# Folding the width once more ahead of a Fourier kernel's first product, in a new order of steps

## The chip, the cores and the metric

One core of one Trainium2 chip. The metric is the device time of one execution in microseconds (us); smaller is better. The engines are named as the profile names them: PE (TensorE, matrix products), DVE (VectorE), ACT (ScalarE), POOL (GpSimd) and SP (SyncE, which here only issues loads).

## The reference

Two heads stand side by side in the output. Head A filters an image of 2048 x 512 in the frequency domain; head B is an FNet layer, the real part of a two-dimensional Fourier transform by given matrices.

```python
# A: x (1, 2048, 512), w_r and w_i (2048, 257)
X = jnp.fft.rfft2(x, axes=(-2, -1))
a = jnp.fft.irfft2(X * (w_r + 1j * w_i), s=(2048, 512), axes=(-2, -1))
# B: x (1, 2048, 512), four DFT matrices given as inputs
p = jnp.einsum("bsd,ed->bse", x, dft_hid_re)
q = jnp.einsum("bsd,ed->bse", x, dft_hid_im)
b = jnp.einsum("ts,bse->bte", dft_seq_re, p) - jnp.einsum("ts,bse->bte", dft_seq_im, q)
return jnp.concatenate([a, b], axis=-1)
```

All values are fp32.

## The kernel before

Both transforms are done by products with tables of cosines and sines, and symmetries halve them. For B the kernel uses its own tables, and it reads the given matrices (34 blocks of 1 MB) only to compare them with what they should be; if one differed, a slow path after the main part (`tc.If`) would compute B from the given matrices.

Each piece of work is a named step. A string, `PLAN`, lists all steps in one order, written out by hand; the instructions of PE, DVE, ACT and SP are issued in exactly that order, each engine taking its own steps from it and waiting by semaphores for the others. POOL's stores are not in the manual order: they are issued as soon as what they store is ready, in their own order. The steps:

- A's input: `xa` loads a block of x (SP), transposed so that the width (512) lies on the partitions, as two halves of two parts k of 128. There are eight blocks i of 256 rows, two to a buffer (b = i // 2, c = i % 2). `fold{i}` (DVE, lines 333 to 339) adds and subtracts the two halves (d and d + 256) into `us`; fold0 and fold1 do one block each, fold3, fold5 and fold7 two. `hid{i}` (PE, L347) is the first product, over the width: h = 0 for even and h = 1 for odd frequencies, the two parts k added up in PSUM, for two groups r of 128 rows. Each `mm` of fp32 is run as two passes (a weight load and a matmul each). `zs{i}` (ACT) copies its result out of PSUM, `f16_{i}` (PE, L359) is a transform of length 16 along the sequence, `ys{i}` (ACT) copies that to `fz`.
- A's spectrum, eight slots n, for each: `w` (SP, weights and table), `tr` (PE transposes, L405), `ez` (ACT), `sf` (DVE, L415 to L417), `fwd` (PE, L424 or L428), `prod` (DVE, the product with the weights, L455 to L459), `comb` (DVE, L463 to L467), `inv` (PE, L485 or L488), `ev` (ACT). Slot 2 is a special one (g2, sx2, spec2, spy).
- A's output, eight steps j: `hi` (PE, L520), `eu` (ACT), `g16_` (PE, L532), `sc` (ACT), `eo` (DVE, two instructions, L541), and one store `st` (POOL, L547, 1 MB) for two j.
- B: `xb` loads, `xr` (ACT), `al` (PE, L606 and L607), `av` (ACT), `bh` (PE, L628 to L632), `hv` (ACT), `ro` (PE, L644), `y1` and `y3` (ACT), `y2` (DVE, L659), `pt` (POOL stores); `rx` and `ry` for one row.
- The comparison: `tt` loads a table (1 MB, two buffers), `cl{i}` loads a block of the given matrix (1 MB), `cc{i}` compares (DVE, one instruction of 128 x 2048, L701; cc16 and cc17, for the hidden matrices, four of about 512 each), `sg` (ACT) flips signs in a table between its uses. Each compare leaves a sum in `stat`; after the last step these are added up (`rs`, `pf`, `flag`), and all engines read `flag`.

The blocks that xa, xb and cl load into share one ring of six buffers (`blk`, NB = 6) of 1 MB: a load waits on SP until the block six before it in the order is no longer needed. PSUM holds three tiles of the kind `pa` for A and two of the kind `pb` for B, in the same way.

Of the kernel before, what the change touches and what calls it, by code (L numbers as in the profile page):

```python
# [16 lines left out]
P = 128  # L17
# [125 lines left out]
def _tables():  # L143
# [63 lines left out]
    first = np.concatenate([hf.reshape(2, 128, 512).transpose(1, 0, 2).reshape(128, 1024),  # L207
                            f16.reshape(128, 128), np.eye(128)], 1)
# [15 lines left out]
def kernel(  # L224
# [52 lines left out]
    dve.memset(ones, 1.0)  # L277
    zero = sp.tile([P, 512], mybir.dt.bfloat16, name="zero")
# [31 lines left out]
    def us(b):  # L310
        return part(2048 * (b % 2), 2, 2, 2, 256)

    def forward(i):
# [6 lines left out]
        if i < 4 or c:  # L320
            @step(f"xa{i}")
            def _():
                if c == 0 or i > 3:
                    block(("xs", b))
                if i < 4:
                    load(xs(b)[:, c], xa[0, :, i].rearrange("p r k f -> p r (k f)"))
                else:
                    load(at["xs", b], xa[0, :, i - 1 : i + 1].rearrange("p c r k f -> p (c r k f)"))

        if i < 2 or c:  # L330
            @step(f"fold{i}")
            def _():
                for h, op in enumerate((ADD, SUB)):
                    if i < 2:
                        TT(out=us(b)[:, h, c].rearrange("p k f -> p (k f)"), in0=xs(b)[:, c, 0], in1=xs(b)[:, c, 1],  # L335
                           op=op)
                    else:
                        TT(out=us(b)[:, h].rearrange("p c k f -> p c (k f)"), in0=xs(b)[:, :, 0],  # L338
                           in1=xs(b)[:, :, 1], op=op)

        @step(f"hid{i}")
        def _():
            pd = bank_a(("pd", i))
            for r in range(2):
                for h in range(2):
                    for k in range(2):
                        mm(pd[:, r, h], us(b)[:, h, c, k, 128 * r : 128 * r + 128], hf[:, k, h],  # L347
                           start=k == 0, stop=k == 1)
# [159 lines left out]
    def inverse(j):  # L508
# [35 lines left out]
        if half:  # L544
            @step(f"st{quad}")
            def _():
                pool.dma_start(out_a.rearrange("(r p) s -> p r s", p=P)[:, :, 512 * quad : 512 * quad + 512],  # L547
                               ob.rearrange("p r k g s -> p (r k) (g s)"))
# [227 lines left out]
    dve.tensor_reduce(out=rs, in_=stat, axis=mybir.AxisListType.X, op=ADD)
    pf = bank_b("pf")[:, :1]
    mm(pf, ones, rs, start=True, stop=True)
# [122 lines left out]
```

## Time and profile before

| what | value |
|---|---|
| time, median of 3 runs | 205.94 us (204.54 to 206.11) |
| the profiled execution | 205.54 us |
| its span in the profile | 203.4 us |
| PE busy | 182.2 us (90%) |
| DVE busy | 155.6 us (76%) |
| ACT busy | 83.6 us (41%) |
| POOL busy | 23.0 us (11%) |
| moved by DMA | 66.24 MB, mean 326 GB/s |
| granted clock of PE, mean | 0.961 |

How to read it: an instruction's row names its line in the kernel, its engine, and output <- input. PE's own time is not the sum of its instructions' durations, since they overlap; the distance between two starts is what one costs. The chain of waits goes back from the end of the execution to whatever released each instruction, and so names what set the time. A granted clock of 1.00 is PE's full clock; 0.50 is half of it.

### The profile page before, as it was taken

The numbers are of one execution on the slowest core, as the hardware profiler recorded it, in microseconds if no ns is written. First come the engines' busy times: TensorE is split into PE (matmuls) and PEld (weight loads), VectorE is DVE, ScalarE is ACT, GpSimd is POOL, SyncE is SP. The second block draws the span as 40 slices with busy tenths as digits, with TensorE's granted clock in tenths as the row PEclk, the third lists the DMA queues.
The fourth block names the chain that finished last, engine by engine and source line by source line (L and its number), as shares of the span: only waits on it lengthen the run. The fifth ranks groups of instructions, "written<-read, shape, count | busy, mean of one in ns | idle before, by whom it ended". The sixth has DMA issues, their size and how long they took to land.

```text
span 203.4 us, 2751 instructions
## 1 busy us (share of the span) xinstructions
PE 182.2 (90%) x1017; PEld 156.5 (77%) x1017; DVE 155.6 (76%) x217; ACT 83.6 (41%) x114; POOL 23.0 (11%) x32
## 2 busy tenths in 40 slices
PE   7299999999999999898999995799999999999810
PEld 2189999999996998788956853777787999999700
DVE  0454049915997899999999999946499997999770
ACT  2003555677864356425332352154344436141400
POOL 5000000000100000000000022303352423101010
PEclk9999999999999999999999999599999999999965
DMA  6999999999999996779599029398999999999241
GB/s 197 396 417 412 427 376 421 401 413 406 398 413 405 407 388 233 255 270 358 148 337 338 29 58 356 153 338 310 428 352 395 367 416 421 421 419 414 114 174 47
DMA packets 19603, 66.24 MB, mean 326 GB/s; under 512 B 1760, under 2 KB 2656, under 8 KB 18688
## 3 DMA queue, kind: packets, MB, share of 16 engines
q1 hardware_dynamic: 16784, 56.33, 72.4%
q0 software_dynamic: 2656, 9.08, 11.4%
q10 hardware_dynamic: 144, 0.59, 0.9%
q8 instruction: 10, 0.16, 0.3%
q14 instruction: 9, 0.07, 0.1%
HBM read 57.61 MB, written 8.39 MB: 325 GB/s over the span
## 4 chain that ended last, share of the span: by engine, by line
PE 58%; DVE 34%; DMA 3%; issue 2%; POOL 0%; ACT 0%; DVEq 0%; ACTq 0%; POOLq 0%
PE pa L347 15%; PE pa L520 14%; DVE work L459 9%; DVE blk L701 8%; PE pa L532 7%; PE pa L359 7%; DMA wsp_sb<-in_wsp 3%; PE pb L644 3%; DVE work L463 3%; DVE work L465 3%; PE pb L632 3%; DVE work L466 2%; DVE work L464 2%; PE pa L485 2%; DVE work L415 2%
## 5 line engine op out<-in xcount | busy, mean ns | idle before, releaser
L701 DVE SCALAR_TENSOR_TENSOR blk<-blk,tt 128x2048 f32<-128x2048 f32 (+2 forms) x24 | 41.4, 1754 | 2.8 <-ACT tt L741 2.3
L701 DVE SCALAR_TENSOR_TENSOR blk<-blk,odd,tt 128x2048 f32<-128x2048 f32 x16 | 37.1, 2346 | 6.6 <-DMA blk<-in_cm 6.6
L347 PE MATMUL pa<-ta,work 128*128 128x256 f32 x128 | 31.1, 401 | 3.7 <-DVE work L335 3.7
L347 PEld LDWEIGHTS pa<-ta,work 128*128 128x128 f32 x128 | 25.4, 203 | 8.1 <-DVE work L335 4.6
L520 PE MATMUL pa<-ta,fz 128*128 128x256 f32 x128 | 29.5, 386 | 0.0
L520 PEld LDWEIGHTS pa<-ta,fz 128*128 128x128 f32 x128 | 28.9, 305 | 0.4 <-issue 0.2
L485 PE MATMUL pa<-fi,work 128*128 128x128 f32 x112 | 15.8, 300 | 4.8 <-DVE work L467 3.8
L485 PEld LDWEIGHTS pa<-fi,work 128*128 128x128 f32 x112 | 14.8, 211 | 6.0 <-DVE work L467 4.2
L459 DVE TENSOR_TENSOR work<-pa,w 128x1024 f32<-128x1024 f32 x14 | 16.5, 1219 | 2.3 <-PE pa L424 1.6
L352 ACT COPY work<-pa 128x1024 f32<-128x1024 f32 x8 | 8.1, 1012 | 24.1 <-PE pa L347 24.1
L363 ACT COPY fz<-pa 128x1024 f32<-128x1024 f32 x8 | 15.3, 1942 | 3.6 <-PE pa L359 3.6
L338 DVE TENSOR_TENSOR work<-blk 128x1024 f32<-128x1024 f32 x6 | 7.1, 1221 | 12.7 <-PE pa L347 12.7
L525 ACT COPY work<-pa 128x1024 f32<-128x1024 f32 x8 | 8.1, 1013 | 20.8 <-PE pa L520 20.8
L359 PEld LDWEIGHTS pa<-ta,work 128*128 128x128 f32 x128 | 15.4, 192 | 0.4
L359 PE MATMUL pa<-ta,work 128*128 128x128 f32 x128 | 15.4, 275 | 0.0
L532 PEld LDWEIGHTS pa<-ta,work 128*128 128x128 f32 x128 | 15.1, 192 | 0.2
L532 PE MATMUL pa<-ta,work 128*128 128x128 f32 x128 | 15.1, 275 | 0.0
L541 DVE TENSOR_TENSOR work<-pa,work 128x512 f32<-128x512 f32 x16 | 10.3, 684 | 6.2 <-ACT work L536 6.2
L606 PE MATMUL pb<-fb,blk 128*128 128x200 f32 (+1 forms) x64 | 14.6, 309 | 0.0
L607 PE MATMUL pb<-fb,xr 128*128 128x200 f32 (+1 forms) x64 | 14.6, 309 | 0.0
L492 ACT COPY fz<-pa 128x1024 f32<-128x1024 f32 x8 | 8.1, 1011 | 12.6 <-PE pa L485 9.5
L424 PE MATMUL pa<-work,fi 128*128 128x512 f32 x28 | 12.8, 592 | 0.0
(94 smaller groups left out, 240.7 us busy)
## 6 DMA issues: line engine op xcount, KB each, us to landing
blk<-in_cm SPq DMA_DIRECT2D x32, 1024.0 KB, 11.1
tt<-tab_tt SPq DMA_DIRECT2D x4, 1026.0 KB, 15.4
w<-in_wa SPq DMA_DIRECT2D x8, 512.0 KB, 9.2
out_a<-work POOLq DMA_DIRECT2D x4, 1024.0 KB, 8.6
blk<-in_xb SPq DMA_DIRECT2D x15, 256.0 KB, 7.9
blk<-in_xa SPq DMA_DIRECT2D x4, 512.0 KB, 7.2
blk<-in_xa SPq DMA_DIRECT2D x2, 1024.0 KB, 11.1
blk<-in_wd SPq DMA_DIRECT2D x2, 1024.0 KB, 6.8
```

Source lines behind the costliest of these rows:

```text
L347: mm(pd[:, r, h], us(b)[:, h, c, k, 128 * r : 128 * r + 128], hf[:, k, h], start=k == 0, stop=k == 1)
L359: mm(y[:, r, c], zs[:, r, 128 * c : 128 * c + 128], f16, start=True, stop=True)
L363: act.copy(fz.rearrange("p c k (n g) -> p g (c k n)", g=16)[:, i::8], flat(at["py", i]))
L424: mm(flat(px[:, h]), ft[:, 0], flat(t[:, h]), start=True, stop=True)
L459: TT(out=m[:, h].rearrange("p i (r q) f -> p i r (q f)", r=2), in0=x2, in1=w2, op=MUL)
L485: mm(pi[:, i, q], lhs[i], it[:, 0], start=True, stop=True)
L520: mm(pu[:, k, h], gz[:, 2 * h + q, 2 * j + k], at["di"][:, h, q], start=q == 0, stop=q == 1)
L532: mm(po[:, k, q // 2, q % 2], u[:, k, q], at["g16"], start=True, stop=True)
L541: TT(out=ob[:, r, :, 2 * half : 2 * half + 2].rearrange("p k j s -> p j k s"), in0=at["po", j][:, :, 0], in1=sc, op=op)
L606: mm(bank[:, lo : lo + w], x[:, g, k], fb[:, n // 15, 0, :w], start=True, stop=False)
L607: mm(bank[:, lo : lo + w], xr[:, g, k], fb[:, n // 15, 1, :w], start=False, stop=True)
L701: dve.scalar_tensor_tensor(raw, raw, k, v, op0=MUL, op1=ALU.not_equal, accum_out=stat[:, i : i + 1])
```

## The change

Ahead of A's first product the width is folded twice. The first fold is as before, but x is loaded from the second copy in `xa`, in which the second part of each half is in mirrored order (row 128 first, then 255 down to 129); sums and differences go to `us`, which is now one buffer used by DVE alone, and of those the two parts of 128 (d and 256 - d) are added and subtracted again into `vs` (double-buffered, read by PE). For the odd frequencies the second fold is two `scalar_tensor_tensor` instructions with a scalar per partition (`but0`: 1 and -1, but 0 in partition 0), for the even ones two plain ones. fold{i} thus has six DVE instructions instead of two. hid{i} has, for each r, two products with 128 columns (odd), one with 256 and one with 129 that adds to it (even), instead of four with 256. Its table shrinks from 1024 columns to 641.

All steps stand in another order. The sum of the comparison's results (rs, pf, flag) is now made of steps too, which stand at the end of the plan, with the last two stores between them. The store of the last quarter of A (1 MB) is split into two halves, st30 and st31 (256 columns of the sequence each); st30 needs only eo6.

The table-building lines of the diff and the two index lines of `first` are left out below.

```diff
@@ -21,21 +21,21 @@
 TINY = 2.0**-111
 SLOTS = [1, 2, 0, 3, 4, 5, 6, 7]
 PLAN = """
-xa0 we xa1 xa2 xa3 xa5 xa7 cl0 cl1 fb fold0 hid0 bt fold1 tt0 cl2 fold3 hid1 zs0 cl3 tt1 f16_0 zs1 fold5 hid2
-ys0 cl4 f16_1 zs2 w0 hid3 ys1 f16_2 zs3 fold7 w1 hid4 ys2 cc0 xb0 cc1 f16_3 zs4 xb1 hid5 cc2 ys3 xb2 cc3 f16_4
-zs5 xb3 cc4 sg0 hid6 ys4 cl5 cl6 cl7 cl8 xb4 f16_5 zs6 xb5 xb6 hid7 xb7 xr0 ys5 cc5 f16_6 zs7 f16_7 w2 cc6 ys6
-al0 ys7 late cc7 al1 av0 tr0 av1 tr1 sg1 cc8 tr2 ez0 ez1 al2 sf0 al3 av2 sf1 fwd0 xb8 av3 xb9 xb10 xb11 cl9
-cl10 xr1 cl11 cl12 fwd1 prod0 ez2 fwd2 comb0 w3 prod1 tr3 g2 al4 ez3 al5 comb1 av4 w4 inv0 av5 sx2 al6 ev0 sf3
-al7 spec2 av6 cc9 cl13 inv1 av7 xr2 tr4 ev1 prod2 fwd3 ez4 comb2 al8 w5 al9 av8 al10 sf4 av9 spy al11 cc10
-av10 inv2 xb12 av11 xb13 xb14 xb15 cl14 prod3 cl15 fwd4 ev2 comb3 w6 tr5 xr3 tr6 prod4 ez5 al12 ez6 al13 av12
-comb4 inv3 av13 sf5 al14 w7 ev3 al15 sf6 av14 inv4 av15 cc11 fwd5 ev4 cc12 cl16 tt2 fwd6 prod5 cl17 tr7 bh8
-ez7 comb5 bh0 hv8 prod6 inv5 hv0 ro0 comb6 ev5 bh1 y10 sf7 y20 inv6 hv1 cc13 y30 fwd7 ev6 cc14 cl18 cl19 rx
-ro1 ry prod7 y11 cl20 bh2 pt0 comb7 hv2 y21 inv7 cc15 y31 pt1 ro2 ev7 bh3 cc16 cl21 tt3 y12 hi0 hv3 y22 cl22
-sg2 y32 cc17 pt2 ro3 eu0 bh4 cl23 tt4 y13 y23 g16_0 y33 hv4 pt3 ro4 sc0 bh5 eo0 y14 y24 hi1 cc18 hv5 y34 pt4
-cc19 cl24 ro5 eu1 bh6 cc20 y15 cl25 g16_1 hv6 y25 cl26 cc21 y35 ro6 sc1 pt5 bh7 y16 eo1 cl27 sg3 hi2 y26 hv7
-st0 cc22 y36 pt6 cc23 cl28 ro7 eu2 hi3 y17 cc24 cl29 y27 g16_2 cl30 eu3 cc25 y37 g16_3 sc2 pt7 eo2 cl31 sg4
-hi4 cc26 sc3 eo3 cl32 hi5 eu4 cc27 st1 cc28 cl33 g16_4 eu5 g16_5 cc29 sc4 hi6 sc5 eo4 eo5 cc30 st2 hi7 eu6
-cc31 g16_6 eu7 cc32 g16_7 sc6 eo6 sc7 eo7 cc33 st3
+xa0 xa1 xa2 xa3 tt0 cl0 xa5 xa7 we fb fold0 cl1 fold1 tt1 hid0 bt fold3 cl2 hid1 zs0 f16_0 zs1 cc0 xb0 hid2
+ys0 xb2 fold5 f16_1 zs2 xb3 f16_2 ys1 xb1 hid3 ys2 cl3 cc1 hid4 zs3 fold7 cl4 f16_3 zs4 f16_4 ys3 hid5 ys4 cl5
+cl6 cc2 hid6 zs5 w0 f16_5 zs6 cl7 xr0 hid7 ys5 w1 cc3 al0 zs7 f16_6 av0 cc4 sg0 f16_7 ys6 w2 cc5 al1 ys7 late
+al2 av1 cc6 tr0 av2 tr1 ez0 tr2 sf0 ez1 al3 sf1 fwd0 xb4 av3 cc7 xb7 ez2 xb6 xb5 fwd1 xb8 cl8 prod0 sg1 tr3
+xb9 xb10 comb0 fwd2 cl9 xb11 xb12 prod1 xb13 xr1 xb14 g2 al4 comb1 ez3 inv0 av4 cl10 sx2 al5 w3 ev0 al6 sf3
+av5 spec2 al7 cc8 av6 w4 inv1 av7 xr2 prod2 tr4 xb15 ev1 al8 ez4 cc9 al9 av8 cl11 al10 av9 sf4 w5 al11 av10
+comb2 fwd3 av11 cl12 cl14 xr3 cl13 fwd4 cc10 spy al12 al13 prod3 av12 al14 av13 al15 cc11 av14 w6 inv2 cl15
+av15 cl16 cc12 tt2 cl17 comb3 bh8 cl19 ev2 bh0 hv8 prod4 inv3 hv0 comb4 tr5 w7 ev3 tr6 ez5 cc13 ro0 ez6 cc14
+inv4 y10 bh1 ev4 y20 cl18 cl20 sf5 y30 rx sf6 tr7 hv1 ry bh2 cc15 ez7 pt0 ro1 hv2 cc16 tt3 fwd5 y11 cl21 ro2
+y21 cl23 sg2 fwd6 sf7 y12 y31 y22 bh3 pt1 prod5 y32 fwd7 hv3 pt2 comb5 bh4 prod6 ro3 hv4 inv5 y13 comb6 ro4
+ev5 y23 inv6 y14 prod7 y33 bh5 pt3 ev6 y24 comb7 y34 bh6 hv5 pt4 ro5 hv6 cc17 inv7 y15 bh7 ev7 y25 cl22 tt4
+cc18 y35 ro6 hv7 pt5 hi0 y16 cc19 cc20 cl24 cl25 hi1 eu0 cc21 cl26 g16_0 y26 eu1 cl27 cc22 sg3 hi2 sc0 y36
+cc23 pt6 hi3 eo0 eu2 cl28 cl29 cc24 g16_1 cc25 cl32 ro7 eu3 cc26 cl30 g16_2 y17 sc1 sg4 hi4 eo1 cl31 sc2 y27
+st0 eo2 y37 pt7 hi5 cc27 eu4 cc28 cl33 g16_3 cc29 hi6 sc3 eu5 cc30 g16_4 eo3 cc31 g16_5 st1 eu6 sc4 hi7 sc5
+eo4 eo5 cc32 st2 g16_6 eu7 cc33 g16_7 sc6 sc7 eo6 eo7 st30 rs st31 pf flag
 """
 
 
...
@@ -275,6 +278,10 @@
 
     ones = const("ones", P)
     dve.memset(ones, 1.0)
+    but0 = const("but0", 2)
+    dve.memset(but0[:, 0:1], 1.0)
+    dve.memset(but0[:, 1:2], -1.0)
+    dve.memset(but0[0:1, :], 0.0)
     zero = sp.tile([P, 512], mybir.dt.bfloat16, name="zero")
     dve.memset(zero, 0.0)
     fz = const("fz", 4, 16, 128)
@@ -287,10 +294,10 @@
 
 
 
-    tf = const("ta", 1152, src=tabs["first"][:, :1152], by=act)
-    hf = tf[:, :1024].rearrange("p (k h f) -> p k h f", k=2, h=2)
-    f16 = tf[:, 1024:]
-    eye = const("eye", P, src=tabs["first"][:, 1152:], by=pool)
+    tf = const("ta", 1152)[:, :769]
+    act.dma_start(tf, tabs["first"][:, :769])
+    hd0, hs0, hd1, hs1, f16 = (tf[:, a:b] for a, b in ((0, 256), (256, 385), (385, 513), (513, 641), (641, 769)))
+    eye = const("eye", P, src=tabs["first"][:, 769:], by=pool)
     wsp_sb = const("wsp_sb", 8, 2, 2, 2, src=wsp, by=pool)
     odd = const("odd", 2, src=tabs["odd"], by=pool)
     turn = sp.tile([P, 8], mybir.dt.int32, name="turn")
@@ -307,8 +314,10 @@
     def xs(b):
         return at["xs", b].rearrange("p (c r f) -> p c r f", c=2, r=2)
 
-    def us(b):
+    def vs(b):
         return part(2048 * (b % 2), 2, 2, 2, 256)
+
+    us = part(6144, 2, 2, 2, 256)
 
     def forward(i):
         b, c = divmod(i, 2)
@@ -323,29 +332,37 @@
                 if c == 0 or i > 3:
                     block(("xs", b))
                 if i < 4:
-                    load(xs(b)[:, c], xa[0, :, i].rearrange("p r k f -> p r (k f)"))
+                    load(xs(b)[:, c], xa[1, :, i].rearrange("p r k f -> p r (k f)"))
                 else:
-                    load(at["xs", b], xa[0, :, i - 1 : i + 1].rearrange("p c r k f -> p (c r k f)"))
+                    load(at["xs", b], xa[1, :, i - 1 : i + 1].rearrange("p c r k f -> p (c r k f)"))
 
         if i < 2 or c:
             @step(f"fold{i}")
             def _():
-                for h, op in enumerate((ADD, SUB)):
-                    if i < 2:
-                        TT(out=us(b)[:, h, c].rearrange("p k f -> p (k f)"), in0=xs(b)[:, c, 0], in1=xs(b)[:, c, 1],
-                           op=op)
+                own = slice(c, c + 1) if i < 2 else slice(0, 2)
+                for h, op in ((1, SUB), (0, ADD)):
+                    TT(out=us[:, h, own].rearrange("p c k f -> p c (k f)"), in0=xs(b)[:, own, 0],
+                       in1=xs(b)[:, own, 1], op=op)
+                    lo, hi = us[:, h, own, 0], us[:, h, own, 1]
+                    diff, plus = vs(b)[:, h, 1, own], vs(b)[:, h, 0, own]
+                    if h:
+                        dve.scalar_tensor_tensor(diff, hi, but0[:, 1:2], lo, op0=MUL, op1=ADD)
+                        dve.scalar_tensor_tensor(plus, lo, but0[:, 0:1], hi, op0=MUL, op1=ADD)
                     else:
-                        TT(out=us(b)[:, h].rearrange("p c k f -> p c (k f)"), in0=xs(b)[:, :, 0],
-                           in1=xs(b)[:, :, 1], op=op)
+                        TT(out=diff, in0=lo, in1=hi, op=SUB)
+                        TT(out=plus, in0=lo, in1=hi, op=ADD)
 
         @step(f"hid{i}")
         def _():
             pd = bank_a(("pd", i))
+            v = vs(b)[:, :, :, c].rearrange("p h g (r f) -> p h g r f", r=2)
             for r in range(2):
-                for h in range(2):
-                    for k in range(2):
-                        mm(pd[:, r, h], us(b)[:, h, c, k, 128 * r : 128 * r + 128], hf[:, k, h],
-                           start=k == 0, stop=k == 1)
+                mm(pd[:, r, 1, 0], v[:, 1, 1, r], hd1, start=True, stop=True)
+                mm(pd[:, r, 1, 1], v[:, 1, 0, r], hs1, start=True, stop=True)
+            for r in range(2):
+                even = pd[:, r, 0].rearrange("p q f -> p (q f)")
+                mm(even, v[:, 0, 1, r], hd0, start=True, stop=False)
+                mm(even[:, :129], v[:, 0, 0, r], hs0, start=False, stop=True)
 
         @step(f"zs{i}")
         def _():
@@ -541,11 +558,17 @@
                 TT(out=ob[:, r, :, 2 * half : 2 * half + 2].rearrange("p k j s -> p j k s"),
                    in0=at["po", j][:, :, 0], in1=sc, op=op)
 
-        if half:
+        to = out_a.rearrange("(r p) s -> p r s", p=P)
+        if quad == 3:
+            @step(f"st3{half}")
+            def _():
+                lo = 256 * j
+                pool.dma_start(to[:, :, lo : lo + 256],
+                               ob[:, :, :, 2 * half : 2 * half + 2].rearrange("p r k j s -> p (r k) (j s)"))
+        elif half:
             @step(f"st{quad}")
             def _():
-                pool.dma_start(out_a.rearrange("(r p) s -> p r s", p=P)[:, :, 512 * quad : 512 * quad + 512],
-                               ob.rearrange("p r k g s -> p (r k) (g s)"))
+                pool.dma_start(to[:, :, 512 * quad : 512 * quad + 512], ob.rearrange("p r k g s -> p (r k) (g s)"))
 
     for j in range(8):
         inverse(j)
@@ -768,15 +791,23 @@
                 half, tb = divmod(j, 4)
                 compare(18 * q + 8 * half + 4 * mt + tb, k, q, mt, half, tb)
 
+    rs = const("rs", 1)
+
+    @step("rs")
+    def _():
+        dve.tensor_reduce(out=rs, in_=stat, axis=mybir.AxisListType.X, op=ADD)
+
+    @step("pf")
+    def _():
+        mm(bank_b("pf")[:, :1], ones, rs, start=True, stop=True)
+
+    @step("flag")
+    def _():
+        dve.tensor_scalar(flag, at["pf"][:, :1], 0.0, None, op0=ALU.is_equal)
+
     for name in PLAN.split():
         steps.pop(name)()
     assert not steps, steps
-
-    rs = const("rs", 1)
-    dve.tensor_reduce(out=rs, in_=stat, axis=mybir.AxisListType.X, op=ADD)
-    pf = bank_b("pf")[:, :1]
-    mm(pf, ones, rs, start=True, stop=True)
-    dve.tensor_scalar(flag, pf, 0.0, None, op0=ALU.is_equal)
     written.close()
     first.close()
     small = nc.values_load(flag[0:1, 0:1], min_val=0, max_val=1)
```

More of the change, by code (lines that the diff above doesn't have):

```diff
@@ L175, in _tables @@
     fb, mb, hc, turn = _tables_b()
-    d = np.arange(256)
-    hf = np.zeros((256, 2, 2, 128))
-    for h in range(2):
-        th = _ang(np.outer(d, _freqs(h)), D)
-        hf[:, h, 0], hf[:, h, 1] = np.cos(th), -np.sin(th)
-    hf[:, 0, 1, 0] = np.cos(np.pi * d)
+    hf = np.zeros((128, 641))
+    th = _ang(np.outer(np.arange(128), _freqs(0)), D)
+    hf[0, 64:128] = 1.0
+    hf[:, 128:256] = -np.sin(th)
+    hf[:, 256:384] = np.cos(th)
+    hf[0, 320:384] = 0.0
+    hf[:, 384] = np.cos(np.pi * np.arange(128))
+    th = _ang(np.outer(np.arange(128), _freqs(1)), D)
+    hf[:, 385:513], hf[:, 513:] = np.cos(th), -np.sin(th)
+    hf[0, 513:] = -np.sin(np.pi / 2 * _freqs(1))
     a = np.arange(16)
@@ L206, in _tables @@
     di /= S * D
-    first = np.concatenate([hf.reshape(2, 128, 512).transpose(1, 0, 2).reshape(128, 1024),
-                            f16.reshape(128, 128), np.eye(128)], 1)
+    first = np.concatenate([hf, f16.reshape(128, 128), np.eye(128)], 1)
     late = np.concatenate([di.reshape(128, 1024), g16], 1)
@@ L343, in _ @@
             pd = bank_a(("pd", i))
+            v = vs(b)[:, :, :, c].rearrange("p h g (r f) -> p h g r f", r=2)
             for r in range(2):
-                for h in range(2):
-                    for k in range(2):
-                        mm(pd[:, r, h], us(b)[:, h, c, k, 128 * r : 128 * r + 128], hf[:, k, h],
-                           start=k == 0, stop=k == 1)
+                mm(pd[:, r, 1, 0], v[:, 1, 1, r], hd1, start=True, stop=True)
[4 more added lines that the diff above has]
+                mm(even[:, :129], v[:, 0, 0, r], hs0, start=False, stop=True)
         @step(f"zs{i}")
```

## The prediction, made before the changed kernel was run

> **What bounds the kernel now.** I read the page's busy shares first, then the chain of waits in order of time, then the busy time by windows, to see what is full at each place.
>
> ```profile
> span 203.4 us, 2751 instructions
> PE 182.2 (90%) x1017; PEld 156.5 (77%) x1017; DVE 155.6 (76%) x217; ACT 83.6 (41%) x114; POOL 23.0 (11%) x32
> ```
>
> The shares alone would say PE. The chain (start, length, what) says that the bound changes twice:
>
> ```profile
> 8.37 0.61 DVE work L335
> ...
> 9.02 9.39 PE pa L347 x32
> 18.41 1.78 PE pa L359 x16
> 20.20 3.46 PE pa L347 x16
> ...
> 53.43 0.34 PE pb L606 x2
> ...
> 54.10 0.25 PE pb L606 x2
> ...
> 55.76 2.62 PE pa L405 x24
> ...
> 60.72 1.73 PE pa L424 x4
> ...
> 78.44 0.10 DVE w L455
> ...
> 81.02 0.69 DVE work L463
> 81.71 0.61 DVE work L464
> ...
> 83.85 0.60 DVE work L415
> ...
> 85.24 2.26 DVE blk L701 x2
> 87.50 0.10 DVE w L455
> ...
> 117.65 0.74 DVE yb L659 x2
> ...
> 128.17 0.18 DVE work L467
> ...
> 128.39 3.79 PE pa L485 x16
> ...
> 139.43 0.86 PE pb L644 x2
> 140.29 0.43 PE pb L628 x2
> ...
> 141.57 1.06 PE pb L632 x4
> ...
> 170.85 7.25 PE pa L520 x32
> 178.10 3.57 PE pa L532 x32
> ...
> 193.69 0.68 DVE work L541
> 194.37 2.22 DVE blk L701 x2
> 196.61 0.21 DVE rs L776
> ...
> 197.49 0.16 DVE flag L779
> ```
>
> From 9 to 60.7 us every piece is PE, back to back: hid (L347) and f16 (L359) in turn, then al and tr. From 62.5 to 128.35 every piece is DVE: prod, comb, sf and compares. From 128.4 to 192.4 it is PE again: ro, bh, hi, g16. The end is DVE: eo7, the last compare, rs, flag. Each engine is idle only where the other is full: the room is in spreading the work, and in making less of it.
>
> ```profile
> 57.91 0.69 DVE L415 TENSOR_TENSOR work<-pa,work 128x512 f32<-128x512 f32 x1
> ```
>
> That is sf0, where I cut the first part off; comb7 ends at 128.35, the second cut; the last eo ends at 194.37, the third. So before: 57.9, then 70.4, 66.0 and 9.0 us; the profiled execution lies 2.14 us above its span (205.54 against 203.4), and 0.4 below the median of 205.94.
>
> **The change, part by part: prices.** A pass of PE takes 3.46/16 = 0.216 us with 256 columns and 1.78/16 = 0.111 with 128. hid had 16 passes of 256. Now each r has four passes of 128, two of 256 and two of 129: 4 x 0.111 + 2 x 0.216 + 2 x 0.112 = 1.10, for both r **2.20 us instead of 3.46**; eight times, 10.1 us less PE. al is 2 x (0.34 + 0.25) = 1.17, a tr 2.62/3 = 0.87, bh 0.43 + 0.43 + 0.42 + 1.06 = 2.34, ro 0.86, hi 7.25/2 = 3.6, g16 1.78.
>
> On DVE a slot's prod and comb take 78.44 to 83.85 = 5.41, sf 1.39, a compare 2.26, y2 0.74. The new fold instructions are no other kinds than these:
>
> ```profile
> L338 DVE TENSOR_TENSOR work<-blk 128x1024 f32<-128x1024 f32 x6 | 7.1, 1221 | 12.7 <-PE pa L347 12.7
> L701 DVE SCALAR_TENSOR_TENSOR blk<-blk,tt 128x514 f32<-128x514 f32 x4 | 2.8, 694 | 2.3 <-ACT tt L741 2.3
> L659 DVE TENSOR_TENSOR yb<-yb,pb 128x255 f32<-128x255 f32 x12 | 4.5, 412 | 1.3 <-ACT yb L653 1.3
> ```
>
> fold0 and fold1 get four instructions of 256 elements each (0.41, and 0.74/2 = 0.37 when nothing is waited for): 1.5 us more, 2.8 in all. fold3, 5 and 7 get four of 512 (0.69, or 0.61): 2.6 more, 5.0 in all. Together **10.8 us more DVE**: what PE saves, DVE pays. The pointer scalar instead of a number costs at most 60 ns each (2346 against 2285 ns at 2048 elements), 0.6 in all.
>
> [...]
>
> **Up to sf0.** DVE folds earlier than anything else now: fold0 8.3 to 11.1, fold1 to 13.9, fold3 to 18.7. hid2's even half (1.3 us) can only follow that, so hid2 ends at 20.1: here PE waits about 2 us for DVE, and the clock's slow start is hidden behind it. Then nothing stops PE: seven f16 (12.5), hid3 to 7 (11.0), al0 to 2 (3.5): 47.1; tr0 48.0; ez0 0.6: **48.6**. fold5 (ready 25.9) and fold7 (33.1) are in time, though tt0 and cl0 now go ahead of xa5 and xa7 on SP: xa5 is the 5.7th MB in the queue, lands about 19 and is wanted at 21. ACT copies 1.0 and 1.9 us per block beside PE's 4.0; its one new wait is sg0 for cc3 (41), with ys6 and ys7 queued behind it, which want to start at 43.
>
> The loads are the other condition. DMA is full here, and in the old order compares waited for it:
>
> ```profile
> 40.00:50.00 10.00, 10.00 (x62) 9.17 (x61) 3.97 (x4) 7.27 (x8) 0.00 (x0) 1.00 1.04 409
> ...
> 47.53 2.35 DVE L701 SCALAR_TENSOR_TENSOR blk<-blk,odd,tt 128x2048 f32<-128x2048 f32 x1 [5.92 <-DMA blk<-in_cm]
> ...
> 55.69 2.29 DVE L701 SCALAR_TENSOR_TENSOR blk<-blk,tt 128x2048 f32<-128x2048 f32 x1 [0.30 <-DMA blk<-in_cm]
> ...
> blk<-in_cm SPq DMA_DIRECT2D x32, 1024.0 KB, 11.1
> ```
>
> Adding up the loads' sizes in the old order, 17.6 MB are asked for up to cl5 (used at 47.5) and 20.7 up to cl8 (55.7), at 0.41 MB per us (409 GB/s). In the new order it is 17.1 MB up to cl6: 0.5 MB earlier than cl5 was, so it lands about 46.4, and cc6 ends at **48.7**, as good as together with PE's 48.6. sf0 starts at 48.7, against 57.9: **-9.2 us**. cl7 (50.5) and w0 (48) are there before cc7 and prod0 want them.
>
> **From sf0 to comb7.** Counted in the new plan, DVE does 8 slots (43.3), seven sf (9.7), sx2 (1.4), cc7 to cc15 (20.3), the hidden compare cc16 (4 x 0.69 = 2.8) and y20 to y24 (3.7): **81.2**. Counted in the old plan it did six compares, no hidden one and one y2: 68.8, and the trace shows 70.4, so such a sum has held within 1.6 us. It ends at 129.9: **+10.8**, because three compares, cc16 and four y2 have come in from the two other parts. PE has 70 us of work in it: fwd0 to 7 (seven of 1.73, fwd2 3.5: 15.6), al3 to 15 (15), inv0 to 6 (14), tr3 to 7 (4.4), six or seven bh (15), ro0 to 4 (5.6). I followed the slots one by one: fwd is done before prod wants it every time, since a compare stands between sf and prod or another slot does; waits for PSUM tiles (fwd2 behind prod0, inv0 behind prod1) stop PE for 1 to 2 us, with DVE busy all the while.
>
> **From comb7 to the last eo.** DVE: cc17 2.8, y25 to y27 2.2, sixteen compares 36.2, eight eo at 1.3: **51.6**, so 181.5. PE, from about 126.9: bh6, bh7, ro5 to 7, inv7 and 8 x 5.35: 51.7, so 178.6, and eo7 can't be before 180.5. The two come out together, so a delay of either counts nearly in full. Before it was 66.0: **-14.4**. The old part also held a slow clock (last columns: granted clock, DMA share, GB/s), which doubled inv7 to 3.79 us and cost 2.5 in all, after PE had waited 3.8 us for comb7:
>
> ```profile
> 127.00:128.00 1.00, 0.00 (x0) 0.00 (x0) 1.00 (x2) 0.00 (x0) 0.00 (x0) 0.50 1.03 422
> ```
>
> Now bh5 and bh6 stand there, and PE waits less than 2 us.
>
> **The end.** Before, eo7 was followed by cc33, rs, pf and flag (197.65), and 5.75 us later the program ended. The store:
>
> ```profile
> 194.66 0.75 POOL L547 DMA_DIRECT2D out_a<-work  x1 [9.94 <-DVE work L541]
> ...
> DMA to landing us min/median/max: 4.6/8.6/11.4
> ```
>
> It landed at 199.3 at the earliest, and 4.1 us followed. Now flag comes 1.1 us after eo7 (196.6 to 197.65 as before): 6.9 instead of 9.0, **-2.1**. POOL issues the two halves one behind the other (0.75 us each), the first behind eo6; the whole MB took 4.6 us from its issue, so they land about 5 us behind eo7, before flag's 6.9 is over. If the end hung on the store, it would be 5 + 4.1 = 9.1: no gain. I take the flag, since its chain is the later one. [...] No row here shows a half store.
>
> **Sum**: 203.4 - 9.2 + 10.8 - 14.4 - 2.1 = 188.5; with 2.14 around the span 190.6, and 191.0 as a median. Nothing is in this for two engines that hand work to each other with no slack; I add 1 us: **192.0**. The floor is DVE without any idle time: 8 + 36.7 (we, folds, seven compares) + 81.2 + 51.6 + 6.9 + 2.5 = 187.
>
> **Rivals.**
> 1. *The loads bound the last part.* Before, DMA was full from 140 to 190, and compare blocks only come free one by one (six buffers). At 130 us there are cl22, tt4, cl24 to cl33 (12.6 MB) and about 5.5 MB of stores to move by cc33: 18.1 MB at 0.41 = 44 us, of 48. cl30 is the tightest: queued behind cl32, it lands by this count at 161 to 164 and is wanted at 165.6. Each block that comes late costs up to 2.6 us; with three late, 196 to 201. Against it: cl18 to cl21 and cl23 are in before comb7.
> 2. *Hand-over waits.* PE and DVE each stop the other for 0.5 us in each of 8 slots and 8 inverse steps: +8, 196 to 200. For: PE is 86% full beside DVE. Against: the old middle part lost 1.6 us in all.
> 3. *The short passes save nothing*, because 16 weight loads per hid remain: 10 us back, 201 to 203. Against: L359's 0.111 us with the same weights' size, half of 0.216.
> 4. *Slower: the clock stays low in the middle part.* If PE waits there as before comb7 (3.8 us), it then runs at 0.50 for about 7 us and loses 3.5. PE has 11 us of slack, so three such waits are free; eight, one per slot, cost 28 - 11 = 17: 209. From the seventh on, the kernel is slower than before. Against: the longest wait that I find is under 2 us. [...]
>
> **Chances.** Forecast (188 to 196) 0.70, rival 1 0.12, rival 2 0.09, rival 3 0.03, within 1% 0.03 (several of these at once), rival 4 0.03. A 1% change, 2 us, is about what this kernel's runs can tell (204.54 to 206.11). The range goes from just above the floor into rivals 1 and 2: 188 to 199.
>
> **What would show it.** hid at 2.2 us; sf0 at 48.7, with cc6 in front of it waiting for its load; DVE over 95% busy from 49 to 182, 166 us in all; PE near 172; granted clock 1.0 throughout after 14 us; comb7 at 130; eo7 at 182; the end 6.9 us behind it. The forecast is wrong if DVE is found waiting for blocks after 140 us, or for PE in the slots, or if the cold clock comes back.

## The result: 192.5 us instead of 206.0, and the profile after

The changed kernel takes **192.51 us** (median of four runs, 192.35 to 192.64), the kernel before 206.03 beside it. The ratio is **0.9358**, with a 95% interval of 0.9313 to 0.9403: 13.5 us faster. A second comparison, on another chip, gave 192.86 us and 0.9416 (0.9381 to 0.9451). Two single executions far off all others (one of the kernel order alone, below, with 380.8 us, and one of the kernel before with 1047.7) are left out of all readings. The profiled execution took 192.64 us with a span of 190.3, so 2.34 lie around the span.

From the profile of the changed kernel come the busy shares, the granted clock in 40 slices (tenths of full speed), and the shares of the chain that ended last:

```profile
span 190.3 us, 2768 instructions
PE 169.9 (89%) x1017; PEld 147.1 (77%) x1017; DVE 166.3 (87%) x240; ACT 83.9 (44%) x114; POOL 23.6 (12%) x33
PEclk9999999999999999999999999999999999999985
DVE 52%; DMA 35%; issue 7%; SPq 1%; POOL 1%; DVEq 0%; POOLq 0%
```

PE lost 12.3 us of work and DVE gained 10.7: the work has been made less and moved. PE is gone from the chain. What is left there is DVE, and transfers that DVE waits for in a few places. Three pieces of the chain in order of time (start, length, what) show where:

```profile
13.30 20.61 DMA blk<-in_cm
...
33.93 2.37 DVE blk L724 x2
36.32 15.76 DMA blk<-in_cm
...
52.11 2.30 DVE blk L724 x2
...
152.33 15.15 DMA blk<-in_cm
...
167.58 2.30 DVE blk L724 x2
```

A DMA piece here runs from a load's issue to its landing; all of it is charged to the chain, though DVE worked beside most of it. What counts is how long the compare behind it stood, which the timeline of DVE gives in brackets. This is its first part, the folds and the road to sf0 (line 432):

```profile
7.78 0.69 DVE L344 TENSOR_TENSOR work<-blk 128x512 f32<-128x512 f32 x1
8.50 0.48 DVE L349 SCALAR_TENSOR_TENSOR work<-work,but 128x256 f32<-128x256 f32 x1
8.90 0.48 DVE L350 SCALAR_TENSOR_TENSOR work<-work,but 128x256 f32<-128x256 f32 x1
...
13.61 1.22 DVE L344 TENSOR_TENSOR work<-blk 128x1024 f32<-128x1024 f32 x1
14.87 0.75 DVE L349 SCALAR_TENSOR_TENSOR work<-work,but 128x512 f32<-128x512 f32 x1
...
18.66 2.29 DVE L724 SCALAR_TENSOR_TENSOR blk<-blk,tt 128x2048 f32<-128x2048 f32 x1
...
38.92 2.29 DVE L724 SCALAR_TENSOR_TENSOR blk<-blk,tt 128x2048 f32<-128x2048 f32 x1 [2.62 <-DMA blk<-in_cm]
...
41.59 2.29 DVE L724 SCALAR_TENSOR_TENSOR blk<-blk,tt 128x2048 f32<-128x2048 f32 x1 [0.37 <-DMA blk<-in_cm]
...
44.03 2.35 DVE L724 SCALAR_TENSOR_TENSOR blk<-blk,odd,tt 128x2048 f32<-128x2048 f32 x1
...
46.54 2.35 DVE L724 SCALAR_TENSOR_TENSOR blk<-blk,odd,tt 128x2048 f32<-128x2048 f32 x1
...
48.81 0.69 DVE L432 TENSOR_TENSOR work<-pa,work 128x512 f32<-128x512 f32 x1
...
52.11 2.29 DVE L724 SCALAR_TENSOR_TENSOR blk<-blk,tt 128x2048 f32<-128x2048 f32 x1 [0.42 <-DMA blk<-in_cm]
...
54.60 1.23 DVE L476 TENSOR_TENSOR work<-pa,w 128x1024 f32<-128x1024 f32 x1
```

fold0 begins at 7.8, fold3 is over at 18.66, sf0 starts at 48.81 (before 57.91) and prod0 at 54.6 (before 62.47). The compares at 38.92, 41.59, 44.03 and 46.54 are cc3 to cc6: cl3 to cl6 land at 38.9, 41.6, 44.0 and 46.5, and each compare starts as its load lands. The short passes of hid are in PE's timeline; this is hid3, sixteen passes from 23.35 to 25.56 and hid4 right behind it (2.21 us instead of 3.46):

```profile
23.35 0.39 PE L360 MATMUL pa<-ta,work 128*128 128x128 f32 x2
...
24.68 0.39 PE L365 MATMUL pa<-ta,work 128*128 128x129 f32 x2
...
25.56 0.39 PE L360 MATMUL pa<-ta,work 128*128 128x128 f32 x2
```

The windows answer to those of before (busy time of PE, PEld, DVE, ACT, POOL, then granted clock, DMA share, GB/s):

```profile
40.00:50.00 10.00, 10.00 (x84) 10.00 (x83) 9.34 (x10) 8.21 (x9) 0.53 (x1) 1.00 1.03 416
...
127.00:128.00 1.00, 1.00 (x6) 0.61 (x4) 0.97 (x3) 0.81 (x2) 0.39 (x1) 1.00 0.64 234
...
160.00:170.00 10.00, 10.00 (x62) 9.95 (x61) 7.59 (x9) 2.02 (x3) 1.55 (x1) 1.00 1.03 421
```

From 127 to 128, where PE had stood still at half the clock, it now works at full clock. From 160 to 170 DVE is busy for only 7.59 us of ten, with DMA full. The reason, and the end, on DVE:

```profile
167.58 2.29 DVE L724 SCALAR_TENSOR_TENSOR blk<-blk,tt 128x2048 f32<-128x2048 f32 x1 [2.41 <-DMA blk<-in_cm]
...
180.14 2.48 DVE L558 TENSOR_TENSOR work<-pa,work 128x512 f32<-128x512 f32 x4
182.54 0.18 DVE L798 TENSOR_REDUCE rs<-stat 128x1 f32<-128x40 f32 x1
183.20 0.16 DVE L806 TENSOR_SCALAR flag<-pb 128x1 int32<-128x1 f32 x1 [0.47 <-PE pb L802]
```

The compare that waited 2.41 us is cc30; its load lands at 167.5. Set against the prediction's cuts (us):

| cut | before | predicted | after |
|---|---|---|---|
| sf0 starts | 57.9 | 48.7 | 48.8 |
| comb7 ends | 128.35 | 129.9 | 129.4 |
| last eo ends | 194.4 | 181.5 | 182.6 |
| span ends | 203.4 | 188.5, with 1 us for hand-over 189.5 | 190.3 |

### The profile page after: what moved, and what is told of

Same layout as the page of the kernel before. It is cut to its first block, busy times and chain, and to the rows that moved or that the text cites. A ratio compares the mean times of both kernels' runs of the same rounds, so it can differ in the third digit from the quotient of the medians.

```text
span 190.3 us, 2768 instructions
## 1 busy us (share of the span) xinstructions
PE 169.9 (89%) x1017; PEld 147.1 (77%) x1017; DVE 166.3 (87%) x240; ACT 83.9 (44%) x114; POOL 23.6 (12%) x33
## 3 DMA queue, kind: packets, MB, share of 16 engines
q0 software_dynamic: 2672, 9.08, 12.3%
## 4 chain that ended last, share of the span: by engine, by line
DVE 52%; DMA 35%; issue 7%; SPq 1%; POOL 1%; DVEq 0%; POOLq 0%
DMA blk<-in_cm 27%; DVE blk L724 24%; DVE work L476 7%; DMA tt<-tab_hs 5%; DMA wsp_sb<-in_wsp 3%; DVE work L558 3%; DVE work L482 2%; DVE work L480 2%; DVE work L483 2%; DVE work L481 2%; DVE yb L682 2%; DVE work L433 2%; DVE work L432 2%; DVE work L344 1%; DVE work L682 1%
## 5 line engine op out<-in xcount | busy, mean ns | idle before, releaser
L502 PEld LDWEIGHTS pa<-fi,work 128*128 128x128 f32 x112 | 13.4, 192 | 4.5 <-DVE work L484 2.6
L549 PEld LDWEIGHTS pa<-ta,work 128*128 128x128 f32 x128 | 15.3, 192 | 1.8 <-PE pa L549 1.2
L502 PE MATMUL pa<-fi,work 128*128 128x128 f32 x112 | 13.8, 276 | 2.4 <-DVE work L484 1.8
L369 ACT COPY work<-pa 128x1024 f32<-128x1024 f32 x8 | 8.1, 1013 | 15.8 <-PE pa L365 15.7
L376 PEld LDWEIGHTS pa<-ta,work 128*128 128x128 f32 x128 | 14.7, 192 | 0.0
L629 PEld LDWEIGHTS pb<-fb,blk 128*128 128x128 f32 x64 | 10.8, 190 | 0.5 <-issue 0.5
L630 PEld LDWEIGHTS pb<-fb,xr 128*128 128x128 f32 x64 | 10.8, 190 | 0.0
L441 PEld LDWEIGHTS pa<-work,fi 128*128 128x128 f32 x28 | 5.1, 190 | 7.1 <-issue 6.8
## 6 DMA issues: line engine op xcount, KB each, us to landing
blk<-in_cm SPq DMA_DIRECT2D x32, 1024.0 KB, 12.3
```

Source lines behind the costliest of these rows:

```text
L369: act.copy(zs, flat(at["pd", i]))
L376: mm(y[:, r, c], zs[:, r, 128 * c : 128 * c + 128], f16, start=True, stop=True)
L441: mm(flat(px[:, h]), ft[:, 0], flat(t[:, h]), start=True, stop=True)
L502: mm(pi[:, i, q], lhs[i], it[:, 0], start=True, stop=True)
L549: mm(po[:, k, q // 2, q % 2], u[:, k, q], at["g16"], start=True, stop=True)
L629: mm(bank[:, lo : lo + w], x[:, g, k], fb[:, n // 15, 0, :w], start=True, stop=False)
```

## The experiments

**Which half of the change does it?** Two kernels each do one of the two large parts.

*Order alone*: the new order and the store in halves, with the fold and hid of before.

```diff
-    tf = const("ta", 1152)[:, :769]
...
+    tf = const("ta", 1152, src=tabs["first"][:, :1152], by=act)
+    hf = tf[:, :1024].rearrange("p (k h f) -> p k h f", k=2, h=2)
+    f16 = tf[:, 1024:]
...
```

The tables, the fold and hid are those of before, line for line; the plan stays that of the changed kernel.

> The changed kernel with the new order and the split store kept, but the fold and hid of before (two fold instructions, 16 passes of 256 columns in hid). Theory (up to sf0 PE, DVE and the loads end within 0.5 us of one another, so giving PE its 10.1 us back makes PE alone the bound there): PE takes 9.0 + 2.5 (cold start) + 41.9 (hid, f16) + 3.5 (al0 to al2) + 0.9 (tr0), ez0 0.6, so sf0 starts at 58.4 instead of 48.8, prod0 at 63.5 instead of 54.4, and everything behind moves with it: 201 to 202 us. Rival 1 (the loads are what holds prod0, through cl7): at most 2 to 3 us more, 194 to 196. Rival 2 (the sum of all DVE work is the bound, and 10.8 us of it go): 192 or less.

Measured: 202.1 us (median of 201.87, 202.10 and 202.65; 206.05 before beside it), ratio 0.9833 (0.9767 to 0.9898), so 3.9 us faster than before. DVE's timeline of this kernel:

```profile
58.60 0.69 DVE L415 TENSOR_TENSOR work<-pa,work 128x512 f32<-128x512 f32 x1 [8.22 <-ACT work L409]
...
63.86 2.35 DVE L459 TENSOR_TENSOR work<-pa,w 128x1024 f32<-128x1024 f32 x2
```

sf0 stands ready with its loads and waits 8.22 us for ez0, which ACT copies from PE's tr0: without the second fold PE is late. The theory held (sf0 at 58.6 where 58.4 was expected, prod0 at 63.9 where 63.5 was), and the time is 0.1 above the range.

*Fold alone*: the second fold and the short hid, with the order of before and one last store.

```diff
-xa0 xa1 xa2 xa3 tt0 cl0 xa5 xa7 we fb fold0 cl1 fold1 tt1 hid0 bt fold3 cl2 hid1 zs0 f16_0 zs1 cc0 xb0 hid2
+xa0 we xa1 xa2 xa3 xa5 xa7 cl0 cl1 fb fold0 hid0 bt fold1 tt0 cl2 fold3 hid1 zs0 cl3 tt1 f16_0 zs1 fold5 hid2
...
-        if quad == 3:
...
-        elif half:
+        if half:
             @step(f"st{quad}")
```

The whole plan is that of before.

> The second fold and the short hid passes, but all steps in the order of before and the last store in one piece; rs, pf and flag stand at the end as before. Theory (in the old order sf0 stands behind cc8, whose load lands at 55.7 whatever PE does): sf0 stays at 57.9, prod0 where it was, the middle and last part as before: 205 to 207 us, with PE waiting some 8 us ahead of fwd0. Rival (PE was the bound up to sf0, so 10 us less of it are 8 to 10 us gained): 196 to 198.

Measured: 202.64 us, ratio 0.9847 (0.9799 to 0.9895), 3.4 us faster than the same 206.05. I had expected 205 to 207, no change, so this was a **miss by 2.4 us or more**. Its DVE timeline:

```profile
47.25 2.35 DVE L718 SCALAR_TENSOR_TENSOR blk<-blk,odd,tt 128x2048 f32<-128x2048 f32 x1 [6.45 <-DMA blk<-in_cm]
...
56.95 0.69 DVE L432 TENSOR_TENSOR work<-pa,work 128x512 f32<-128x512 f32 x1
...
60.52 2.35 DVE L476 TENSOR_TENSOR work<-pa,w 128x1024 f32<-128x1024 f32 x2 [0.63 <-PE pa L441]
```

The loads do hold sf0, as expected (56.95 instead of 57.91). What I had left out is that before, prod0 stood 1.62 us more for fwd0, which PE reached only at 60.55:

```profile
62.47 2.35 DVE L459 TENSOR_TENSOR work<-pa,w 128x1024 f32<-128x1024 f32 x2 [1.62 <-PE pa L424]
```

That is a row of before. With less hid, PE has fwd0 at 58.52, so prod0 comes 1.95 us earlier, and the rest of the run keeps it. The profiled executions are 2.1 us apart (205.54 and 203.47); the interval of the ratio allows 2.2 to 4.1 us, and no trace here shows where the rest of the medians' 3.4 comes from. The slow inv7 is unchanged, in PE's timeline of the same kernel:

```profile
126.00 3.79 PE L502 MATMUL pa<-fi,work 128*128 128x128 f32 x16 [3.75 <-DVE work L484]
```

Now cut the spans of all four kernels at prod0:

| kernel | up to prod0 | from prod0 to the span's end |
|---|---|---|
| before | 62.5 | 140.9 |
| fold alone | 60.5 (-2.0) | 140.8 (-0.1) |
| order alone | 63.9 (+1.4) | 135.9 (-5.0) |
| both | 54.6 (-7.9) | 135.7 (-5.2) |

The profiled execution of fold alone was the slowest of its four (the median is 202.64), so its row may be up to 1 us too long, and what follows holds to within 1 us. Order alone has the store in halves too; the experiments on the end, below, price that at 0.45 us.

**Behind prod0 the order does all of it; ahead of prod0 neither does anything like 7.9 alone**: the fold runs into the loads, the order runs into PE. Only with both gone does DVE come forward. Alone the fold gives 3.4 us and the order 3.9; together they give 13.5.

**What bounds each stretch now?** Three kernels each leave one compare out on DVE, with its load and all else kept: cc4 ahead of sf0, cc9 between sf0 and comb7, cc24 behind comb7.

```diff
         @step(f"cc{i}")
         def _():
+            if i == 4:
+                dve.memset(stat[:, i - 2 * (i > 15) : i - 2 * (i > 15) + 1], 0.0)
+                return
```

> The changed kernel without the DVE instruction of cc4 (a compare of the part up to sf0; its block is still loaded, its sum is set to zero). Theory (DVE waits for the loads there: 2.6 us for cl3, and cc5 and cc6 follow their loads at once): no change, within 0.3 us of the changed kernel's 192.5 to 192.9. Rival (DVE's sum is the bound everywhere): 2.3 us faster.

> The changed kernel without the DVE instruction of cc9 (a compare between sf0 and comb7; its block is still loaded, its sum is set to zero). Theory (DVE bounds the middle part; inv6 waits 1.75 us for comb6, and PE is full from there to the end): 1.7 to 2.3 us faster, 190.4 to 191.1. Rival (PE sets the time there, too): no change.

> The changed kernel without the DVE instruction of cc24 (a compare of the last part; its block is still loaded, its sum is set to zero). Theory (in the last part PE is full and cc30 waits for cl30, so DVE's work is not the bound): at most 0.5 us faster. Rival (DVE is the bound there): 2.3 us faster, 190.3.

| left out | us | ratio (interval) |
|---|---|---|
| nothing | 192.86 | 0.9416 (0.9381 to 0.9451) |
| cc4 | 192.84 | 0.941 (0.9355 to 0.9465) |
| cc9 | 190.42 | 0.9281 (0.9226 to 0.9336) |
| cc24 | 192.64 | 0.9395 (0.934 to 0.945) |

The first row is the second comparison; the other three ran on another chip. By the ratios to the kernel before, leaving out cc4 or cc24 can't be told from leaving out nothing, and leaving out cc9 can. All three came out as the theories had it: the same 2.3 us of DVE are worth nothing, all, and next to nothing. In the trace without cc9 the stretch from sf0 to comb7 takes 78.5 us instead of 80.6. In the first, DVE's timeline shows the wait only moved:

```profile
44.33 2.35 DVE L724 SCALAR_TENSOR_TENSOR blk<-blk,odd,tt 128x2048 f32<-128x2048 f32 x1 [2.68 <-DMA blk<-in_cm]
```

So the **loads** set sf0 (49.04 there), **DVE** sets the middle, and in the last part **DVE, PE with ACT, and the loads** take turns. Without cc24, the wait for ACT at eo1 grows from 0.75 to 3.02 us, which is all that was taken out:

```profile
155.67 1.29 DVE L558 TENSOR_TENSOR work<-pa,work 128x512 f32<-128x512 f32 x2 [3.02 <-ACT work L553]
...
167.71 2.29 DVE L724 SCALAR_TENSOR_TENSOR blk<-blk,tt 128x2048 f32<-128x2048 f32 x1 [2.14 <-DMA blk<-in_cm]
```

**cc30's late load.** The plan asks for cl32, cl30, cl31 in this order, and cc30 is wanted first. One kernel asks for them in turn:

```diff
-cc23 pt6 hi3 eo0 eu2 cl28 cl29 cc24 g16_1 cc25 cl32 ro7 eu3 cc26 cl30 g16_2 y17 sc1 sg4 hi4 eo1 cl31 sc2 y27
+cc23 pt6 hi3 eo0 eu2 cl28 cl29 cc24 g16_1 cc25 cl30 ro7 eu3 cc26 cl31 g16_2 y17 sc1 sg4 hi4 eo1 cl32 sc2 y27
```

> The changed kernel with the last loads in the order in which they are used: cl30, cl31, cl32 in the places of cl32, cl30, cl31. cc30 waits 2.4 us for cl30 at 165.1. Theory (that wait delays eo3, for which PE waits 1.0 us, and PE is full otherwise): cl30 lands 2.5 us earlier, the wait goes, PE gains its 1.0 us and the end comes 0.8 to 1.2 us earlier, 191.3 to 191.7. Rival 1 (DMA is full there, so the wait only moves to cc31 or cc32): no change. Rival 2 (DVE alone is the bound): 2.4 us faster, 190.1.

Measured: 191.33 us, ratio 0.9339 (0.9305 to 0.9372), 1.5 less than the changed kernel beside it (192.86, on the same chip), and within the 191.3 to 191.7 expected. DVE's timeline:

```profile
165.15 2.29 DVE L724 SCALAR_TENSOR_TENSOR blk<-blk,tt 128x2048 f32<-128x2048 f32 x1
...
171.92 2.48 DVE L558 TENSOR_TENSOR work<-pa,work 128x512 f32<-128x512 f32 x4 [1.00 <-ACT work L553]
...
178.80 2.48 DVE L558 TENSOR_TENSOR work<-pa,work 128x512 f32<-128x512 f32 x4
```

cc30 starts without a wait, and of the 2.41 us, 1.0 come back as a wait for sc: eo7 ends at 181.3 instead of 182.6. The late load cost 1.3 to 1.5 us; for the rest of the 2.4, ACT's copy behind PE is the next to be late.

**The end.** After flag is read, every engine branches on it. Two theories: the end follows the flag, or it follows the last store. One kernel stores quad 3 whole, as before:

```diff
-eo4 eo5 cc32 st2 g16_6 eu7 cc33 g16_7 sc6 sc7 eo6 eo7 st30 rs st31 pf flag
+eo4 eo5 cc32 st2 g16_6 eu7 cc33 g16_7 sc6 sc7 eo6 eo7 st3 rs pf flag
```

Another sends the halves from SP, whose queue the function load uses:

```diff
-                pool.dma_start(to[:, :, lo : lo + 256],
+                load(to[:, :, lo : lo + 256],
```

> The changed kernel with its last store in one piece of 1 MB behind eo7. Theory (the end hangs on the landing of the last store, with some 4 us behind it: 199.3 to 203.4 before, 186.4 to 190.3 after): issued at 182.9 and landed 4.6 us later, 187.5 instead of 186.4, so 1.1 us slower, 193.4 to 193.9. Rival, as the prediction had it (the end hangs on flag): no change, 192.4 to 192.6.

> The changed kernel with st30 and st31 issued from SP's queue instead of POOL's. SP issues a load in 0.4 us where POOL takes 0.75 for a store. Theory (the store's landing sets the end): 0.4 to 1.2 us faster, down to what flag allows (183.4 + 5.75, 1.2 us less): 191.3 to 192.1. Rival (flag): no change.

| last store | us | ratio (interval) | flag's end to span's end |
|---|---|---|---|
| halves, POOL | 192.86 | 0.9416 (0.9381 to 0.9451) | 7.0 |
| whole, POOL | 193.31 | 0.9435 (0.94 to 0.9469) | 7.5 |
| halves, SP | 191.61 | 0.9357 (0.9322 to 0.9392) | 6.05 |

The whole store cost 0.45 us between the medians (193.06 to 193.43 against 192.78 to 193.30, so the runs overlap a little), which neither theory had: 1.1 by the store, 0 by the flag. Part of the 1.1 was a misreading: 186.4 was when the halves' data had stopped moving, while the second half landed at 187.7 and the whole store lands at 188.0, only 0.3 later. SP gained 1.25; its range of gains ended at 1.2, though 191.61 lies in the times expected (191.3 to 192.1). The traces show more. These are the branch of PE's weight-load queue (duration in ns, start) in before, the changed kernel, the whole store and the halves from SP:

```profile
L783 PEldq COMPARE_BRANCH  x1: 3524/3524/3524, 198.7 to 198.7; - x1
```

```profile
L814 PEldq COMPARE_BRANCH  x1: 4264/4264/4264, 184.5 to 184.5; - x1
```

```profile
L808 PEldq COMPARE_BRANCH  x1: 5704/5704/5704, 184.2 to 184.2; - x1
```

```profile
L814 PEldq COMPARE_BRANCH  x1: 3544/3544/3544, 184.7 to 184.7; - x1
```

The DMA queues of the changed kernel, from 184 to 186 and from 186 to 187 (packets, MB, share):

```profile
q0 software_dynamic: 170, 0.63, 95.2%
```

```profile
q0 software_dynamic: 34, 0.07, 23.6%
q8 instruction: 1, 0.02, 6.2%
q14 instruction: 3, 0.02, 6.0%
```

The branch starts at 184.5, but until 186 only the store moves. The packets of the kind "instruction" come from 186.4 to 186.6, as the store's last data go (186.6), and the branch ends 2.2 us behind them, at 188.8. With the whole store everything is later: its data end at 187.4, the last instruction packets come at 187.6, and the branch ends at 189.9. In before the store's data ended at 198.8, right behind the start of the branch, and the instructions came from 199.4, 0.7 us behind that start. SP's halves are still moving when the branch begins, here from 184 to 185:

```profile
q1 hardware_dynamic: 338, 0.35, 102.0%
```

But they are through at 185.3, and the instructions come from 185.4, again 0.7 us behind the branch's start at 184.7. So in these four traces **the instructions move only when the last store's data are all but through, and the branch ends 2.0 to 2.3 us behind them**; the span ends another 1.1 to 1.5 us later. What in the chip orders the two was not measured, and the next kernel shows that the order is not strict. Reading flag differs as well: from flag's end to the first branch behind it there are 0.95 us in before, 1.04 in the changed kernel and 1.15 with the halves from SP, but 0.6 with the whole store and in the next kernel, where the store did not move yet.

Two kernels combine the gains. The first takes the loads in turn, the store from SP, and puts rs, pf and flag ahead of eo7:

```diff
-eo4 eo5 cc32 st2 g16_6 eu7 cc33 g16_7 sc6 sc7 eo6 eo7 st30 rs st31 pf flag
+eo4 eo5 cc32 st2 g16_6 eu7 cc33 rs g16_7 pf sc6 sc7 eo6 st30 flag eo7 st31
```

> The changed kernel with the last loads in the order of their use, st30 and st31 from SP's queue, and rs, pf and flag ahead of eo7. Theory (the end comes 1.3 us behind the later of two: the branch, 3.5 us after the flag is read, and the last store's end plus 2.3 us): flag is read right behind eo7, at 181.3 instead of 183.4; the branch begins at 182.5 and ends at 186.0, and the store ends about 184.0, which gives 186.3; span 187.6, 189.7 to 190.2 us. Rival (the gains of the loads' order and of the store's queue do not add): 191.2 or more.

Measured: 190.87 us, ratio 0.9312 (0.9272 to 0.9353): a **miss**, 0.7 above the range (189.7 to 190.2) and still below the rival's 191.2. The branch now starts at 181.2, between the issues of the two halves (180.57 and 181.9), and takes 4.8 us:

```profile
L814 PEldq COMPARE_BRANCH  x1: 4804/4804/4804, 181.2 to 181.2; - x1
```

This time the instructions move from 183.2 to 183.8 beside the store, which has its full share, as the queues from 183 to 184 show:

```profile
q1 hardware_dynamic: 323, 0.31, 100.2%
q8 instruction: 1, 0.02, 6.5%
q14 instruction: 2, 0.02, 3.9%
```

The branch ends at 186.0 and the second half lands at 186.8, 4.9 us behind its issue, where it took 3.0 to 3.3 in the other two kernels that store from SP. It is the only trace in which the store lands behind the branch's end, and the span ends 2.0 us behind the landing. So **the end follows whichever is later, the branch or the last store**; that it can be the store rests on this one trace.

The second leaves rs, pf and flag behind eo7, as in the changed kernel:

> The changed kernel with the last loads in the order of their use and st30 and st31 from SP's queue; rs, pf and flag stay behind eo7, unlike in the run before. Theory (an earlier flag lets the branch's instruction fetch start while the last store is still moving, and the two slow each other: in the run before the store ended 4.5 us behind its second issue instead of 2.9): without the early flag the two gains of 1.5 and 1.25 us add, 190.0 to 190.4 us. Rival (the gains do not add, whatever flag does): 190.8 to 191.3.

Measured: **190.32 us**, ratio 0.9254 (0.9207 to 0.9302), within the 190.0 to 190.4 expected. Its branch takes 3.4 us, and the two gains add up (1.5 and 1.25 by themselves, 2.2 to 2.5 together):

```profile
L814 PEldq COMPARE_BRANCH  x1: 3424/3424/3424, 183.4 to 183.4; - x1
```

This version beats both kernels: before by 15.7 us, beside it on one chip (205.99), and the changed one by 2.2 to 2.5 (192.51 and 192.86), measured on other chips. The kernel with the early flag ran on yet another chip, and the intervals of the two ratios overlap, so that the early flag costs 0.55 us is indicated, not shown.

## Why the prediction came out right, point by point

- **Prices.** hid was priced at 2.20 us and takes 2.21. fold0 was priced at 2.8 and takes 2.9, fold3 at 5.0 and takes 5.05. The pointer scalar was bounded at 60 ns and adds 60 (0.75 against 0.69 at 512 elements). DVE was to gain 10.8 us and gained 10.7: independent instructions (here the two with the pointer scalar) start 0.40 us apart at 256 elements and 0.67 at 512, sooner than each one's duration (0.48 and 0.75).
- **Up to sf0** (forecast 48.7, measured 48.8). Both conditions were right, the loads and PE, and that they meet. cl6 was to land at 46.4 and landed at 46.5, and cc6 starts with it. The long wait stood earlier, though, at cc3 (2.62 us); cc4 to cc6 then follow their loads with stops of 0.4 us or less. The experiments without cc4 and with the order alone show each bound by itself. cc7's load was called in time and was 0.4 late. What the forecast calls the clock's slow start (in the expectation for order alone, 2.5 us of cold start) is shown as time, not as clock: hid0 takes 4.28 us here (9.04 to 13.32) against hid3's 2.21, and in before hid0 and hid1 take 9.39 together against 3.46 for hid2, while the granted clock reads 1.00 from 5 to 14 us in both.
- **sf0 to comb7** (81.2 forecast, 80.6 measured). DVE is the bound, as the run without cc9 shows. DVE's only stop of more than 0.15 us there is the 0.42 for cl7; all its idle time comes to 2.2 us. Rival 2 (a stop of 0.5 us per hand-over) is thereby refuted: the 1 us that I added for it isn't found here. Rival 4 is too: PE's longest wait for DVE is 1.75 us, and the clock stayed at 1.00. Its about 7 us at 0.50 are what before shows, from 126.2 to 133.0; how long a wait has to be for that, no run shows.
- **comb7 to the last eo** (51.6 forecast, 53.2 measured) is the **first term that was mis-sized**. Rival 1 happened in small: it had named cl30 as the tightest load, and cc30 waited 2.41. My count had it land at 161 to 164, ahead of 165.6 in all cases; it landed at 167.5. By my own sign (DVE waiting for blocks after 140 us) this part of the account was wrong, although the sum came out. One more wait, 0.75 at eo1 for ACT, makes 3.2 of idle time; the sum had 1.5 too much work in it (an eo takes 1.20, not 1.3; a compare 2.21 to 2.27).
- **The end** (6.9 behind eo7 forecast, 7.7 measured) is the **second**. The step "I take the flag, since its chain is the later one" took the branch behind flag as a fixed 5.75 us. It was 7.0, as the branch's instructions moved only when the store ended (186.4 to 186.6, with the branch from 184.5); flag itself came 0.74 us behind eo7, where 1.1 was forecast. The halves landed when I said, at 187.7 (5 us behind eo7 is 187.6). That this is harmless because 6.9 is longer was the wrong step: in the traces the branch is longer where a store is in flight (4.3 us here and 5.7 with the whole store, against 3.5 in before and with the halves from SP). The two halves were 0.45 us faster than the whole store by the medians (192.86 and 193.31), with runs that overlap a little. Their data move from 183.0 to 186.6, those of the whole store from 184.0 to 187.4.
- The two terms are short by 1.6 and 0.8; the middle part was 0.65 too long and the 1 us of hand-over was reserved. That leaves 0.8 us of span, and the time outside the span grew by 0.2. The nearness of 192.0 to 192.5 thus owes something to terms that cancel.
- Rival 3 (the short passes save nothing) is refuted by hid's 2.21 us.
- **The other signs.** DVE is 96% busy from 48.8 to 182.6 and 166.3 us in all, and the clock is at 1.00 from 14 to 183 us, as forecast. PE is 169.9 instead of "near 172": the forecast left in the slow inv7, which took 3.79 us in before and takes 1.95 now.

## What to carry to other kernels

When two resources are full in one stretch, relieving either alone gains little, and the gain of both is no sum (here 3.4 and 3.9 us alone, 13.5 together): cut the spans at a point that all versions share and compare stretch by stretch. To learn which resource bounds a stretch, take one instruction of known length out of it and see whether its time comes back. Ask for loads in the order in which they are wanted (1.5 us here), and count the end of a program from its last store as well as from its last instruction (the queue of that store was worth 1.25 us here).

## What the runs showed of the hardware that I had not expected

- The branch at the program's end takes 3.4 to 3.5 us where the last store's data are through by 0.9 us behind its start, and 4.2 to 5.7 where the store moves longer. A flag that is ready earlier seems not to help if the branch then meets the store (190.87 against 190.32 us, on two chips).
- The same 512 KB store takes SP 0.38 us to issue and 3.0 to 3.3 to land (3.5 and 4.9 where the early branch met it), POOL 0.75 and 3.4 to 4.8; at the program's end that is worth 1.25 us.
- A pass of 129 columns costs as much as one of 128 (in hid3 two passes of either kind start 0.22 us apart), and an odd first column of the table costs nothing either (0.11 us a pass at column 385, as in before at column 1024). The pointer scalar costs 60 ns and no more.
